# Another order of the same pieces: a layer norm, windowed attention and a GELU layer on one core

## The chip, the cores and the metric

The kernel runs on one core of a Trainium2 chip. The core has five engines with instruction streams of their own: TensorE (PE, matmuls), VectorE (DVE), ScalarE (ACT), GpSimd (POOL) and SyncE (SP), which here only issues DMA transfers. The metric is the device time of one execution in microseconds (us), smaller is better; the runs of the kernel before took 209.0 to 210.06 us, median 209.08.

## The reference

The input is x with 2048 rows of 640. It is normalised row by row, and the result goes two ways: through an attention with 32 heads of 20, in which each row looks at itself and seven earlier rows at a distance of two, and through a dense layer of 1536 with a tanh GELU. Both results and x are added.

```
xn = _layernorm(x)                                   # 2048 x 640
q, k, v = split(xn @ wqkv)                           # 32 heads of 20
logits[s, w] = q[s] . k[s - 2 w] * 20 ** -0.5        # w = 0..7, -1e9 where s - 2 w < 0
o[s] = sum over w of softmax(logits)[s, w] * v[s - 2 w]
A = o @ wo
B = gelu(xn @ w1 + b1) @ w2 + b2
return x + A + B
```

## The kernel before

The rows are cut into four chunks (n = 0 to 3) of 512 rows, each of four blocks (bl or j) of 128. Everything is held transposed, with features on the partitions and rows along the free dimension, so that a shift by a row is a shift of an address.

The work of a chunk is cut into pieces, each a small function under a short name. One string, ORDER, lists every piece once; the kernel runs through it and records each piece's instructions, and so each engine gets its instructions in the order of that string. No scheduler moves them later. An engine takes them strictly in that order, and waits at an instruction until its inputs are there and its target buffer is free. The names, with the digit of the chunk first:

- Loads on SP: `ldx` (the x rows of chunks 2 and 3, three transfers), `ld2` (w2, four), `ldo` (wo, three). The loads of chunks 0 and 1, of wqkv and of w1 are issued before the list begins.
- Layer norm: `st` (statistics on DVE, chunks 0 and 1), `su`, `sq` (row sums and squares on ACT, chunks 2 and 3), `rs`, `rc` (reciprocal of the deviation on ACT, mean times it on DVE), `xn` (the normalised rows; on ACT from chunk 1 on). Then `tc` turns a block: by PE and a copy in chunk 0, by a DMA transpose on SP from chunk 1 on (`do_td`).
- Projections: `hj`/`hc` (chunk 0, in pairs of blocks) and `pj`/`pc` (other chunks): `pj` is five matmuls of 512 columns on PE into an accumulator of the pool `psA`, `pc` the copy of it on ACT. The two digits behind the chunk are which of q, k, v (0, 1, 2) and which fifth of the features. `ga`, `gb`, `gd`, `ge` and `gc` are the first q columns, `pad` and `pk` carry 14 columns over from the chunk before.
- Attention on DVE: `qk` multiplies q of one block with the eight shifted k (one instruction of 5120 elements in each partition, 2.8 us), `pa`, `pb` add features up, `lg` sums over heads on PE into a PSUM tile L, `cp` copies it out (for chunk 0 half by ACT, `cp0a`, and half by DVE, `cp0b`), `m`, `mx`, `ex`, `ss`, `ri`, `at` are the softmax (largest value, subtraction, exponent, sum, reciprocal, product; `ex` and `ri` on ACT). `xe` spreads the weights of one block from 32 partitions to 128: a DMA on SP (`expand`), an expansion below. `av` multiplies them with the shifted v (again 2.8 us), `ac`, `ad`, `ot` add the eight positions up (of chunks 0 to 2, blocks 0 and 1 do `ac` by an accumulating DMA on POOL) and give oT.
- Dense layer: `f1` (five matmuls on PE into `psA`), `ge` (bias and GELU on ACT; it needs another table of functions than `ex`, `ri` and `rs`, so a table load of 1.28 us stands where the kind changes).
- Output of chunks 0 to 2: `t` (on PE into the pool `psO`; the last digit 0 to 3 are parts of gelu @ w2, three matmuls each, 4 is o @ wo, five matmuls, which needs oT), `u` (bias, ACT), `ut` (a DMA transpose back on SP, an output transpose below), `ud` (an accumulating DMA on POOL into the output, onto which `xp` has copied x). Chunk 3 is computed with rows on the partitions instead: `o3` (PE; last digit 4 needs oT), `dl`, `dh` (addition of x on DVE), `dd`, `dlo`, `dhi` (stores). `xb` adds b2 to the x rows of chunk 3. `ohi` is a last group of narrow matmuls.

The pool `psA` has four accumulators and serves `hj`, `pj`, `f1` and some of `o3`; `psO` has two and serves `t`. So a `pj` or `f1` on PE waits until ACT has emptied the accumulator that it gets, which is one used about four such pieces earlier.

The lines: 289 is the DMA transpose of `tc`, 125 the load of x rows, 153 of w2, 575 the expansion, 701 the output transpose, 612 `f1`, 331 `pj`, 694 `t`, 650 `o3`, 478 `lg`, 428 `qk`, 463 and 469 `pa` and `pb`, 582 `av`, 595 `ac`, 599 `ad`, 605 `ot`, 218 and 225 `su` and `sq`, 260 `xn`, 395 `pc`, 515 and 518 `cp`, 628 `ge`, 697 `u`, 706 `ud`, 593 `ac` by DMA, 170 the table load. The list is run here:

```
    with tc.manual_schedule(engines=engines):

        do_warm(WARM, CH)
        do_warm(3, P)
        assert sorted(ORDER) == sorted(pieces)
        for name in ORDER:
            pieces[name]()
```

Of the kernel before, what the change touches and what calls it, by code (L numbers as in the profile page):

```python
# [37 lines left out]
COLS = ((0, 2), (2, 4), (4, 5))  # L38

ORDER = """  # L40
sum1 st00a st00 wa rs00 xn00a wb tp00a neg1 xn00b tp00b tc00a tb sq1 ga tc00b rs01 gb2 mean1 xn01a tp01a gb3 xn01b
st03a tc01a st02a st02 tp01b gb4 gd st03 tc01b ge hj100 gc0 rs02 xn02 rs03 gc4 xn03 st11a gc1 hc100 st12a tp02 st13a
st10a tp03 st13 st10 hj102 st11 tc02 st12 tc03 hj101 pad01 hc101 hj111 hj112 hc102 hc111 rs1 rc1 xn13 hc112 pk b1
hj011 xn11 hj110 hj202 hj010 hc011 hc110 hj012 tc13 hc010 qk00 hc202 tc11 xn10 hj200 ldx f10_1 qk01 pa00 f10_2 hc012
qk03 ge0_1 f10_0 qk02 f10_3 ge0_2 xn12 ge0_0 f10_11 f10_5 hc200 ho pa01 ge0_3 ge0_11 tc10 tc12 su20 su22 pb01 f11_3
ge1_3 pj104 pj111 su21 pad11 pad02 pc104 su23 pj101 pc111 pj102 ng2 pc101 pj112 sq22 pj100 ge0_5 pb04 sq21 pj113 pc112
pj114 lg0 pc100 sq23 pc113 pc102 cp0a pj110 pc114 cp0b m0b pj103 xp2 hj210 ld2 hj201 xp0 mask mx0b m0a ex0b pc103 mx0a
pc110 ss0b pj121 sq20 qk10 rs2 hc210 pj122 f10_7 t000 ex0a hc201 ss0a rc2 xp1 f10_9 pc122 ri0b ri0a qk11 pc121 f10_4
ge0_4 su33 ge0_9 qk13 f10_6 t001 pj120 qk12 f11_5 xn23 ge0_7 pj124 ge0_6 su32 pc120 f11_10 xn20 f11_9 ldo t040 ge1_10
f10_8 pc124 su31 tc23 ge0_8 tc20 t041 xn21 hj211 pa10 at0a t002 su30 f11_0 tc21 hc211 xn22 ng3 pa11 at0b ge1_9 sq32  # L50
xe01 f11_1 pb11 t042 ge1_1 pb14 sq30 f10_10 hj212 ge0_10 lg1 t003 sq31 tc22 xe00 av01 cp1a pj202 hc212 pj214 xe02
ge1_0 pj204 ge1_5 sq33 pj210 av00 ac01 pc202 rs3 pc204 pj123 av02 t043 pc210 pj200 pj211 pc214 xe03 ac00 cp1b pc211
rc3 pc123 pj203 pj201 pc201 pj213 pj220 pc203 m1 pad12 mx1 pc200 av03 pad21 ac02 ex1 xn30 pc213 ss1 pj221 pj222 pc220
tc30 pc221 ac03 pj223 xn33 f12_10 ri1 at1 pc222 ad01 pj224 xe10 ad00 xn32 xe13 pc223 ot01 ot00 pj212 xe12 pc212 f11_4
av10 xe11 av12 f11_6 pc224 f11_8 av13 t004 ac10 ac13 tc32 t044 u00 t010 t011 t012 u04 t013 ut00 t014 ud00 av11 t020
xn31 t021 tc31 ac12 u01 t030 t022 ge1_8 t023 tc33 t024 f11_2 t031 ad11 ge1_4 ac11 t032 t033 ge2_10 pad22 ge1_6 t034
pj313 ot11 u03 qk22 pj312 pc313 qk23 pc312 pj324 ut01 ge1_2 ad10 u02 pj303 f11_7 pc324 pc303 ge1_7 t140 pj301 pj310
f12_1 ge2_1 ut02 t141 pc310 ot10 pa21 qk20 t130 f11_11 pj311 pc311 pc301 f12_2 pj304 pc304 qk21 pa20 t131 f13_2 ge1_11
pj300 pb21 pb24 pj302 ge2_2 pad31 pj314 pc302 t132 t142 pc314 t143 f13_8 pc300 f13_10 f12_0 lg2 pad32 t144 qk31 ut03
ut04 ud01 t133 cp2b t134 ud02 ge2_0 ud03 ge3_2 f13_1 cp2a u13 ge3_10 pj320 m2 qk30 t100 pc320 ge3_1 f13_5 qk32 pa30  # L60
t101 u14 ge3_5 xb mx2 f12_11 f12_8 qk33 t110 t111 t102 t112 f12_5 ge2_11 t113 t103 ex2 t104 ge2_5 u10 f12_4 ss2 ri2
ut10 t114 t120 t121 t122 pa31 at2 xe20 xe21 ge2_4 f13_7 pb31 u11 ge3_7 pj322 pc322 f12_3 pb34 f13_6 lg3 ge3_8 f13_4
xe22 ut11 cp3a ge2_3 ge3_6 t230 ge2_8 av21 av22 av20 f12_7 t123 f12_6 ge2_6 pj323 f13_0 ge3_4 xe23 t124 f12_9 pc323
ud10 f13_11 ge2_7 u12 ge3_0 ac21 t200 f13_3 ac20 av23 ge2_9 cp3b m3 mx3 ge3_11 o300 ge3_3 t201 ac22 ac23 ex3 ss3 o320
ri3 o301 ad21 ut12 t202 pj321 ud11 o321 t203 pc321 at3 xe30 ud04 xe31 ut13 o322 t231 t232 ot21 xe32 f13_9 ad20 ge3_9
ut14 ot20 t233 av30 o302 t204 xe33 u20 t234 t210 ut20 av31 t211 t212 o310 u23 t220 t213 t221 ud12 t222 t214 o323 u21
t223 t224 ac31 u22 av33 ac30 t240 o311 t241 av32 t242 ud13 ud20 o312 ad30 ut21 t243 t244 o313 ot30 o330 ud14 ac32 ac33
u24 ud21 ad31 ut22 o314 o331 ud22 o332 o303 o304 o333 ot31 o324 dh0 dl1 dh1 ut23 o334 ut24 ohi dl0 ud23 dh2 dd0 dl2
dl3 dd1 dd2 dh3 dlo ud24 dhi
""".split()  # L70


# [782 lines left out]
```

## Time and profile before

| | |
|---|---|
| median of 3 runs | 209.08 us (209.0 to 210.06) |
| the profiled execution | 209.62 us, its span 207.8 us |
| granted TensorE clock | 1.0 |
| ACT, 40 to 65 us | 23.34 us busy of 25 |
| PE, 40 to 65 us | 24.73 us busy of 25 |
| ACT, 152 to 205 us | 17.09 us busy of 53 |
| x rows, `ldx` (L125), issued | 19.39 us, three in 1.60 us |
| transposes of rows (L289), issue to landing | 2.4 / 4.0 / 6.4 us (least, median, most) |
| expansions (L575), issue to landing | 3.6 / 4.2 / 6.0 us |
| output transposes (L701), issue to landing | 2.3 / 3.3 / 6.2 us |
| loads of x (L125), issue to landing | 2.5 / 4.6 / 8.1 us |

The span runs from the first to the last instruction of the program; the rest of the execution's time lies around it. A row of the timeline gives the start and the duration in us, the engine, the line, what is written from what, a count, and in square brackets how long the engine sat idle before it and what ended that. A `q` behind an engine's name is its sequencer, which issues transfers. Idle time counts only where the engine is the one that the end waits for.

### The profile page before, as it was taken

To read this page: it belongs to the slowest core of one execution; us is meant where nothing else is said; L and a number is where in the kernel's file an instruction comes from. 1 tells how busy PE (TensorE), PEld (TensorE's weight loads), DVE (VectorE), ACT (ScalarE), POOL (GpSimd) and SP (SyncE) were. 2 spreads that over 40 slices of the span, in tenths; PEclk is the share of its full clock that TensorE was granted. 3 is DMA by queue.
4 is the path that set the end of the run, shared out by engine and by line. 5 is a ranking of instruction groups with operands and counts; after the bars stand their busy time and mean duration, and the time that the engine had idled before them with its cause. 6 is when DMAs were issued, how large, how long until landed. Compare 5 with 4: busy or idle time off the path is not lost.

```text
span 207.8 us, 2852 instructions
## 1 busy us (share of the span) xinstructions
PE 199.0 (96%) x1082; PEld 104.9 (50%) x1100; DVE 185.9 (89%) x161; ACT 126.6 (61%) x235; POOL 29.6 (14%) x40
## 2 busy tenths in 40 slices
PE   8999979999999999999999999999999998999793
PEld 3898435564454555444454454444444454444352
DVE  2989999499998998999999997999959999959993
ACT  5679969899989949547272532758964835211100
POOL 2000000000000400031407000000202630207420
PEclk9999999999999999999999999999999999999999
DMA  6996999800219691579597930000495994899963
GB/s 210 391 395 179 271 308 335 317 1 0 65 37 155 153 174 35 123 154 163 101 138 81 100 48 0 3 0 0 82 162 103 138 148 70 137 104 96 106 49 126
DMA packets 38430, 27.31 MB, mean 131 GB/s; under 512 B 25106, under 2 KB 34578, under 8 KB 38418
## 3 DMA queue, kind: packets, MB, share of 16 engines
q1 hardware_dynamic: 28016, 20.39, 39.2%
q0 software_dynamic: 10080, 6.56, 26.5%
q10 hardware_dynamic: 322, 0.20, 0.3%
q8 instruction: 8, 0.13, 0.3%
q14 instruction: 4, 0.03, 0.1%
HBM read 10.49 MB, written 4.59 MB: 73 GB/s over the span
## 4 chain that ended last, share of the span: by engine, by line
PE 50%; DVE 26%; DMA 8%; ACT 6%; SPq 5%; issue 3%; DVEq 0%
PE pps L331 19%; PE T L694 15%; PE hps L612 12%; DVE prod L582 7%; DVE prod L428 5%; DMA x_sb<-in_A_x_dram 4%; SPq L701 3%; DMA x_sb<-attn 3%; PE lo L650 3%; DVE prod L469 2%; DVE prod L463 2%; DVE prod L595 2%; DMA ax<-attn 2%; DVE stats L206 2%; ACT xn L260 1%
## 5 line engine op out<-in xcount | busy, mean ns | idle before, releaser
L612 PE MATMUL hps<-xnT,w_sb 128*128 128x512 bf16 x237 | 56.7, 379 | 1.7 <-ACT trash L218 1.5
L428 DVE TENSOR_TENSOR prod<-qT,kT 128x5120 bf16<-128x5120 bf16 x16 | 44.5, 2820 | 1.4 <-PE L L478 1.3
L694 PE MATMUL T<-hT,w_sb 128*128 128x512 bf16 x177 | 44.4, 379 | 0.2
L612 PEld LDWEIGHTS <-w_sb 128*128 128x128 bf16 x240 | 23.4, 98 | 29.8 <-issue 2.4
L628 ACT ACTIVATE hT<-hps,bT 128x512 bf16<-128x512 f32 x36 | 24.1, 689 | 11.2 <-PE hps L612 9.5
L706 POOL DMA_DIRECT2D out_dram<-x_sb x15 | 20.5, 1613 | 62.6 <-DMA x_sb<-x_sb 62.6
L694 PEld LDWEIGHTS <-w_sb 128*128 128x128 bf16 x180 | 17.2, 98 | 20.2 <-issue 0.4
L697 ACT ACTIVATE x_sb<-T,bT 128x512 bf16<-128x512 f32 x15 | 10.3, 687 | 24.4 <-PE T L694 22.5
L582 DVE TENSOR_TENSOR prod<-vT,x_sb 128x5120 bf16<-128x5120 bf16 x8 | 22.3, 2820 | 3.0 <-DMA x_sb<-attn 3.0
L582 DVE TENSOR_TENSOR prod<-vT,ax 128x5120 bf16<-128x5120 bf16 x8 | 22.1, 2820 | 3.1 <-DMA ax<-attn 2.4
L593 POOL DMA_DIRECT2D prod<-prod x6 | 7.3, 1220 | 106.2 <-DVE prod L582 106.2
L694 PE MATMUL T<-oT,wo 128*128 128x512 bf16 x73 | 17.9, 379 | 0.8 <-DVE oT L605 0.6
L469 DVE TENSOR_TENSOR prod<-prod 128x4096 bf16<-128x4096 bf16 x8 | 18.3, 2290 | 0.2
L463 DVE TENSOR_TENSOR prod<-prod 128x4096 bf16<-128x4096 bf16 x8 | 18.3, 2286 | 0.1
L331 PE MATMUL pps<-xnT,wk_sb 128*128 128x512 bf16 x73 | 18.2, 379 | 0.1
L331 PE MATMUL pps<-xnT,wq_sb 128*128 128x512 bf16 x72 | 18.0, 379 | 0.2
L331 PE MATMUL pps<-xnT,wv_sb 128*128 128x512 bf16 x72 | 17.7, 379 | 0.1
L170 ACT ACT_TABLE_LOAD x12 | 15.4, 1283 | 0.9 <-PEq L839 0.7
L595 DVE TENSOR_TENSOR prod<-prod 128x2560 bf16<-128x2560 bf16 x10 | 14.7, 1485 | 0.1
L331 PEld LDWEIGHTS <-wk_sb 128*128 128x128 bf16 x75 | 8.7, 118 | 7.6 <-issue 0.4
L331 PEld LDWEIGHTS <-wq_sb 128*128 128x128 bf16 x75 | 8.8, 117 | 7.5
L331 PEld LDWEIGHTS <-wv_sb 128*128 128x128 bf16 x75 | 8.8, 117 | 7.3
(96 smaller groups left out, 241.7 us busy)
## 6 DMA issues: line engine op xcount, KB each, us to landing
prod<-prod POOLq DMA_DIRECT2D x6, 640.0 KB, 6.6
ax<-attn SPq DMA_DIRECT2D x8, 256.0 KB, 4.1
x_sb<-attn SPq DMA_DIRECT2D x8, 256.0 KB, 4.6
w_sb<-in_B_w_dram SPq DMA_DIRECT2D x2, 960.0 KB, 11.0
out_dram<-x_sb SPq DMA_DIRECT2D x3, 640.0 KB, 9.3
w_sb<-in_B_w_dram SPq DMA_DIRECT2D x4, 480.0 KB, 7.7
out_dram<-x_sb POOLq DMA_DIRECT2D x15, 128.0 KB, 5.4
x_sb<-in_A_x_dram SPq DMA_DIRECT2D x2, 640.0 KB, 7.2
```

The source lines that it names most:

```text
L170: nc.scalar.preload_act_table_set(name)
L331: nc.tensor.matmul(ps[:], lhsT=wqkv_p[which][:, ti, to, :], rhs=xnT[:, ti, :], start=(ti == 0), stop=(ti == KT - 1),)
L428: nc.vector.tensor_tensor(out=prod[:, j], in0=q[:, :, at].unsqueeze(1).to_broadcast([P, W, KT, P]), in1=window(k, at), op=ALU.mult,)
L463: nc.vector.tensor_tensor(out=low, in0=low, in1=high, op=ALU.add)
L469: nc.vector.tensor_tensor(out=first, in0=first, in1=rows[:, :, t * P : (t + 1) * P], op=ALU.add)
L582: nc.vector.tensor_tensor(out=prod[:, j], in0=window(qkv_tile(n, 2), slice(j * P, (j + 1) * P)), in1=ax_view(n)[:, j, :, :].unsqueeze(2).t ...
L595: nc.vector.tensor_tensor(out=low, in0=low, in1=high, op=ALU.add)
L612: nc.tensor.matmul(ps[:], lhsT=w1_sb[:, ti, ft * P : (ft + 1) * P], rhs=tiles["xnT", n][:, ti, :], start=(ti == 0), stop=(ti == KT - 1),)
L628: nc.scalar.activation(hT, tiles["hps", n, ft][:], ACT.Gelu_apprx_tanh, bias=bT[:, ft : ft + 1], scale=1.0)
L694: nc.tensor.matmul(ps[:], lhsT=lhs, rhs=rhs, start=pc == 0 and k == 0, stop=pc == 4 and k == len(srcs) - 1)
L697: nc.scalar.activation(take("straight", n, s), tiles["T", n, s][:], ACT.Identity, bias=bT[:, FT + s : FT + s + 1])
L706: nc.gpsimd.dma_start(dst, src, accum_op=ALU.add)
```

## The change

ORDER is replaced by another order of the same names. No function, tile, size or buffer is changed, and each engine executes the same instructions but one: the functions' table is loaded once more on ACT (13 times instead of 12). The diff replaces the whole string; what stands in it on the engines that the prediction speaks of is this, each engine's own pieces in their order, old (-) and new (+):

```diff
 SP, first part
-tc13 tc11 ldx tc10 tc12 xp2 ld2 xp0 xp1 ldo tc23 tc20 tc21 xe01 tc22 xe00 xe02 xe03
+tc11 tc13 tc12 tc10 ldx ld2 tc20 xp1 tc23 xe00 xe01 tc21 tc22 xe02 xe03 xp2 xp0 ldo
 SP, second part
-tc30 xe10 xe13 xe12 xe11 tc32 ut00 tc31 tc33 ut01 ut02 ut03 ut04 ut10 xe20 xe21 xe22 ut11 xe23 ut12
+xe10 xe11 xe13 xe12 tc32 tc30 ut00 ut01 tc31 tc33 ut02 ut03 ut04 ut10 xe22 xe20 xe21 ut11 xe23 ut12
-xe30 xe31 ut13 xe32 ut14 xe33 ut20 ut21 ut22 ut23 ut24 dd0 dd1 dd2 dlo
+xe30 xe31 ut13 xe33 ut14 ut20 xe32 ut21 ut22 ut23 ut24 dd1 dd2 dd0 dlo
 ACT, chunk 1's rows
-rs1 xn13 hc112 pk xn11 hc011 hc110 hc010 hc202 xn10 hc012 (table) ge0_1 ge0_2 xn12 ge0_0 hc200 ge0_3 ge0_11 su20 su22
+rs1 hc110 pk xn11 hc111 xn13 hc010 hc011 xn12 hc200 xn10 (table) ge0_11 ge0_2 pad11 ge0_1 hc201 ge0_5 su20 ge0_3 pc110 pc111 su22
 ACT, 39 to 52 us
-cp0a pc114 (table) ex0b pc103 pc110 sq20 rs2 hc210 ex0a hc201 pc122 ri0b ri0a pc121 (table) ge0_4
+cp0a (table) ex0b pc100 pc114 pc101 sq21 ex0a ri0b pc121 pc124 sq23 pc123 ri0a sq20 hc202 rs2 hc210 pc120 (table) ge0_4
 ACT, chunk 3's rows
-xn30 pc213 pc220 pc221 xn33 ri1 pc222 xn32 ... u04 xn31 u01 (table) ge1_8 ge1_4 ge2_10 pad22 ge1_6 u03
+xn32 pc220 pc211 u00 xn30 u04 pad22 xn31 u01 pad31 (table) ge1_2 u03 ge1_7 ge2_1 pad32 xn33 ge1_4
 ACT, last softmax
-(table) ex3 ri3 pc321 (table) ge3_9
+(table) ex3 (table) ge2_9 ge3_3 ge2_11 pc321 pc322 (table) ri3 pc323
 PE, from f10_1 to lg0
-f10_1 f10_2 f10_0 f10_3 f10_11 f10_5 f11_3 pj104 pj111 pj101 pj102 pj112 pj100 pj113 pj114 lg0
+f10_1 f10_11 hj201 f10_2 f10_5 pj110 f10_3 pj102 pj111 pj112 pj103 pj104 f10_0 pj114 pj113 lg0
 PE, the end
-t204 t234 t210 t211 t212 o310 t220 ... t244 o313 o330 o314 o331 o332 o303 o304 o333 o324 o334 ohi
+t204 t234 t210 t211 t212 t220 ... t244 o311 o312 o313 o304 o330 o331 o314 o324 o332 o333 o334 ohi
 DVE, first logits
-pb04 cp0b m0b mask mx0b m0a mx0a ss0b qk10 ss0a rc2 qk11 qk13 qk12 pa10 at0a pa11 at0b pb11 pb14
+pb04 cp0b m0b mx0b mask m0a ss0b mx0a qk13 ss0a qk10 at0b qk11 rc2 qk12 at0a pa11 pa10 pb11 pb14
 DVE, last two chunks
-av21 av22 av20 av23 m3 mx3 ac22 ac23 ss3 ad21 at3 ot21 ad20 ot20 av30 av31 ac31 av33 ac30 av32 ad30 ot30 ac32 ac33 ad31 ot31
+av22 av21 m3 mx3 av20 ss3 ac22 av23 at3 ac23 ad21 ad20 ot21 ot20 av30 av31 ac31 av33 ac30 ad30 av32 ot30 ac33 ac32 ad31 ot31
```

In the list itself `cp0a` stands ahead of `cp0b` before and behind it after. The order on POOL changes in one place: `ud00` is issued ahead of `ac10` instead of behind it.

## The prediction

> **What bounds the kernel now.** I read the page's busy shares first, then the chain of waits, then the timeline around each place where TensorE (PE) stands still, and last the same places on VectorE (DVE), ScalarE (ACT) and the SP queue. From the page:
>
> ```profile
> PE 199.0 (96%) x1082; PEld 104.9 (50%) x1100; DVE 185.9 (89%) x161; ACT 126.6 (61%) x235; POOL 29.6 (14%) x40
> ...
> PE 50%; DVE 26%; DMA 8%; ACT 6%; SPq 5%; issue 3%; DVEq 0%
> ...
> L612 PE MATMUL hps<-xnT,w_sb 128*128 128x512 bf16 x237 | 56.7, 379 | 1.7 <-ACT trash L218 1.5
> ```
>
> A 512-column matmul is shown as 379 ns, but consecutive ones begin closer together, as the chain of waits shows:
>
> ```profile
> 85.35 3.24 PE hps L612 x15
> 88.59 6.69 PE T L694 x31
> ```
>
> 3.24/15 and 6.69/31 are 216 ns each. The same reading of consecutive starts gives 109 ns for 256 columns, 56 ns for 128, and 69 ns per logit matmul. The program issues 788, 125, 118 and 32 of these, beside 24 transposes, bias and late warm-up matmuls: 170.1 + 13.6 + 6.6 + 2.2 + 1.6 = 194.0 us. This total is the same in both kernels, and PE takes it in the written order. So I lay the work ahead of a piece against the moment at which it starts; the difference is the time PE has lost so far. In the trace of before it is 5.5 us at the first transpose, 5.8 at f10_1 (19.96), 7.7 at lg0 (38.04), 7.9 at t004 (88.2), 8.2 at lg2, 8.2 at t204, 8.8 at t244, 10.5 at o314 (195.65) and 10.6 at the end. From t004 to lg3 PE loses 0.4 us in 64. Outside the start, then, it stands still in three places.
>
> PE in the timeline, around 28, 176 and 196:
>
> ```profile
> 28.24 1.02 PE L612 MATMUL hps<-xnT,w_sb 128*128 128x512 bf16 x4 [1.53 <-ACT trash L218]
> ...
> 176.28 1.89 PE L694 MATMUL T<-oT,wo 128*128 128x512 bf16 x8 [0.56 <-DVE oT L605]
> ...
> 195.65 0.39 PE L650 MATMUL lo<-wo,oT 128*128 128x512 bf16 x1 [1.33 <-DVE oT L605]
> ```
>
> The first is f11_3, the first piece that reads all of chunk 1's transposed rows. ACT is named, but its buffer was free at 24.7. What ended last was the fourth transpose. SP and ACT:
>
> ```profile
> 21.10 4.23 SPq L289 DMA_TRANSPOSE xnT<-xn  x2
> ...
> 23.18 0.92 ACT L260 ACTIVATE xn<-x_sb,nmr,rstd 128x640 bf16<-128x640 bf16 x1
> ```
>
> xn12 stands behind a table load and two gelus on ACT, ends at 24.1, and tc12 is issued up to 25.3. The other two places wait for oT from DVE, and DVE itself waits there for expansions stuck behind output transposes on SP:
>
> ```profile
> 177.40 0.60 SPq L575 DMA_DIRECT2D x_sb<-attn  x1
> 178.11 2.16 SPq L701 DMA_TRANSPOSE x_sb<-x_sb  x1
> 180.31 0.59 SPq L575 DMA_DIRECT2D x_sb<-attn  x1
> ...
> 186.30 2.83 DVE L582 TENSOR_TENSOR prod<-vT,x_sb 128x5120 bf16<-128x5120 bf16 x1 [2.19 <-DMA x_sb<-attn]
> ```
>
> **The change, part by part.** Nothing is added but one table load on ACT (1.28 us, the L170 row). The rest is a permutation, so I walk the new order with the durations of the old trace (ACT from start to start: copy 0.47, xn 0.81, gelu 0.57, row sum 0.84, square 0.9; DVE: 2.73 a 5120 product, 2.2 to 2.3 a 4096 one, 1.4 a 2560 one). Where two engines meet I take the later.
>
> *Head, 15 to 36 us.* ACT now runs xn11, xn13, xn12, xn10 ahead of the table load: they end at about 17.1, 18.4, 20.3 and 21.6 with the projection copies between. SP issues tc11, tc13, tc12, tc10 directly behind them (1.2 each), the last up to 22.8. The shortest landing of these transposes is 2.4 us from issue, the longest 6.4. Nothing else loads then, since the x rows wait behind and the w1 halves land before 19; I take 24.0 (by the longest, 28.0). PE reaches pj110, the new first user, at 24.8: the 1.7 us stall goes. By the longest landing 3.2 us come instead. The moved loads (three issues, 1.6 us) go out at 22.8 to 24.4 instead of 19.4 to 21.0, and behind them ld2, tc20 and everything later on SP. Their first reader is su20 on ACT at 26.4; queued behind su20 are ge0_3 and pc110, which free the buffers of pj112 (29.1) and pj103, so rows landing by 27.7 cost nothing. Their landings lie between 2.5 and 8.1 us from issue, that is 25.3 to 30.9; I take the lower part, 27, because these rows now leave right behind the transposes with nothing loading before them.
>
> lg0 thus stands at 29.8 us of work + 5.8 + 0.25 = 35.85, against 38.04. DVE has its input (pb04) at 15.75 + 4x2.73 + 2x2.2 + 2x2.3 = 35.7, so it doesn't hold it. Behind lg0, DVE copies its half before ACT does; before, it came second:
>
> ```profile
> 39.33 0.69 DVE L518 CAST e<-L 128x512 bf16<-128x512 f32 x1 [3.21 <-ACT e L518]
> ```
>
> That is 0.6 us less between logits and softmax.
>
> *Middle, 36 to 152 us.* ACT is the tight one up to 52 (23.34 us busy of 25 in the window 40 to 65). Walking both, f10_4 waits 0.45 us for hc202, f11_10 0.25 us for ge0_4 behind a table load; lg1 stands at 63.5 (before 64.8), pb14 being ready at 63.0. ot00 is ready at 86.4 and t004 wants it at 87.2. Chunk 3's xn33 now waits behind pad32, hence for av11 (98.8): its transpose is issued at 100.9 to 102.1 and lands by 104, or 107.3 by the longest row; pj310 wants it at 105.7, so 0 to 1.6. At lg2 (126.5) DVE is early (pb24 124.7) and idles some 2.5 us: this gives back DVE's lead but costs PE nothing, as PE has other work. lg3 follows at 152.0.
>
> *Tail.* DVE starts on chunk 2's values at 152.6 (before 154.4). m3, mx3 now come between av21 and av20 and at3 ahead of ac23, ad21: at3 ends at 169.0 instead of 173.2. The added table load stands ahead of ri3, behind pc322: pj322 ends at 165.5, copy, load and the two small exponents at 168.0. DVE's av23, up to 168.3, hides it; without that cover at3 would be up to 1.3 us later. xe30, xe31 leave at once, ut13 takes 1.2, xe33 leaves at 171.6 instead of 180.3. DVE wants it at 182.1, and the longest landing of an expansion is 6.0. Only xe32 stays behind ut20, whose source needs t204 and u20: issued by 179.1, landed by 185.1 even at 6.0, wanted at 187.7. Both waits of DVE for expansions go; ot20 ends at 175.0 (t204 wants it at 175.2), ot30 at 191.3 (o304: 192.5), ot31 at 196.5 (o324: 196.5).
>
> **The sum.** PE's loss at the end falls from 10.6 to 5.8 + 0.25 + 0.7 + about 0.5 around the logits and oT = 7.3 us: 3.3 less. Several handovers have under half a microsecond of slack (f10_5, hj202, pj221, ot20, ot31), so I give back 0.7: 2.6 us. If all keep their slack and the 0.5 vanishes too, it is 3.8, hence 205.3; if tc33 and the transposes of chunk 1 take their longest landings, 1.6 + 3.2 eat the gain. The profiled execution took 209.62, span 207.8: it would be 207.0, span 205.2. It stands 0.54 above the median of the runs, 209.08, so the median becomes **206.5**. The tail behind the last matmul (3.1 us) stays.
>
> One rule speaks for another limit: the Trainium skill, "Perfetto Trace Analysis", section "Identifying the Most-Contended Engine", says that busy matmul time tells little and that the share of weight loads should be read. Here that is 50%, so by it PE has room and DVE (89%) is the limit. The 216 ns from start to start, kept for 60 us on end, disagrees.
>
> **Rivals.**
> - *DVE alone is the limit.* Then the end moves as DVE's last oT does: 200.8 to 196.5, so 204.8. For it: DVE's 89%. Against it: PE's work behind that oT grows by o332 and o333 (2x0.65), and PE loses 0.4 us in the middle. 0.06.
> - *The tail's waits return.* xe32 late by over 2.6 us, or t204 and o304 arriving on oT as before, brings back the 0.56 + 1.5: 208.6. For it: ot20 and ot31 have no slack. 0.14.
> - *ACT is overfull between 24 and 52 us.* Each of its delays passes to PE through four accumulator buffers; another 1.5 us there: 208.0. For it: 93% busy. Against it: the walk leaves most copies 0.3 to 1 us early. 0.12.
> - *The later x rows stop ACT: slower.* If the first rows land as the big loads at 29 to 34 us do (9.4 us from issue at most: xp1), su20 waits until 32.8, ge0_3 ends at 34.3, and pj112, due at 29.1, loses 5.2 us, with DVE behind it through lg0: 211.7. It decides from a landing at 30.3 on, where it has eaten the 2.6. Against it: the weight loads are issued behind these rows. 0.11. On this the Trainium skill, "DMA: Bandwidth & Descriptors", section "Queues, rings and completion order", says that each DMA engine takes one queue's descriptors in ring order; by that the weights couldn't overtake. The old order, rows ahead of ld2, shows no wait of su20.
>
> **Chances.** The forecast has 0.57, with 204.8 to 208.0 as its own range. About 0.5% (1.05 us) is what can be told from no change. Faster (under 208.0): 0.55 of the forecast, 0.06, half of ACT's 0.12 and 0.02 of the tail's = 0.69. Slower (over 210.1): 0.11 and 0.01 = 0.12. The same: 0.19. The range 204.8 to 209.4 leaves out the slow rival and a little at the lower end.
>
> **What would show it.** Right: no PE gap over 0.5 us between 24 and 30; lg0 before 36.5; the first copy of L by DVE, without a 3 us wait; an idle DVE of 2 to 3 us before the first product behind lg2; no wait of L582 for x_sb<-attn over 1 us; the last oT before 197.5; SP's expansions of x_sb at 169 to 172. Wrong: su20 (L218 after 26) waiting for x_sb<-in_A_x_dram; a PE gap at the first L331 near 25 or near 105; a wait for oT over 1 us in the last 15 us.

## The result, and the profile after

The changed kernel takes 212.34 us (median of 6 runs, 211.8 to 216.35), the kernel before 209.29 in the runs beside it (208.27 to 210.85). The ratio is 1.0137, 95% interval 1.0092 to 1.0182: slower by 1.4%, where 1.2% faster was forecast.

The first profiled execution of the changed kernel, 216.35 us, was disturbed from its start on, so I read a second one of the same kernel (a0_same, 212.83 us, span 211.1, granted clock 0.983), against the 209.62 us and span 207.8 of before.

> The changed kernel itself, once more. In its trace PE has lost 9.1 us of time by hj101 (5.8 before), stands 4.6 us ahead of pj310 for the transpose tc33, and then runs some 5 us at half the clock. Theory (one late transpose): the head's 3 us belong to that execution alone, so here PE has lost about 6 us at lg0, and 13 to 14 at the end; wait ahead of pj310 4 to 5 us, then starts 432 ns apart; 212.3 us. Rival (the later x loads and the new head cost it): 9 us lost by lg0 again, and most of the difference to before stands ahead of lg0.

Its four executions had a median of 212.41, ratio 1.0157 [1.0103, 1.0210]. From its page: the busy row, the granted clock in 40 slices of 5.3 us, the chain of waits by engine, and two groups of instructions (behind the bar: busy us, mean ns, idle us before them).

```profile
PE 201.9 (96%) x1081; PEld 105.8 (50%) x1100; DVE 186.6 (88%) x161; ACT 128.6 (61%) x236; POOL 29.7 (14%) x40
...
PEclk9999999999999999999975999999999999999999
...
PE 83%; DMA 9%; ACT 3%; DVE 2%; SPq 1%; issue 1%; ACTq 0%
...
L428 DVE TENSOR_TENSOR prod<-qT,kT 128x5120 bf16<-128x5120 bf16 x16 | 44.7, 2820 | 9.1 <-PE L L478 8.9
...
L331 PE MATMUL pps<-xnT,wk_sb 128*128 128x512 bf16 x74 | 19.9, 413 | 4.2 <-DMA xnT<-xn 4.1
```

PE is still 96% busy, and DVE and ACT as before. Three things are new: one idle time of 4.1 us on PE, which a row transpose ended; a clock of 0.7 and 0.5 in the slices 21 and 22 (from 106 us on), where it was 0.9 or more throughout; and 8.9 us in which DVE waited for logits. DVE's part of the chain fell from 26% to 2%: PE alone sets the end now. The place is the first piece that reads chunk 3's transposed rows, pj310. The timeline of PE (start, duration, in brackets the idle time before):

```profile
99.84 5.56 PE L612 MATMUL hps<-xnT,w_sb 128*128 128x512 bf16 x24
109.50 4.43 PE L331 MATMUL pps<-xnT,wk_sb 128*128 128x512 bf16 x10 [4.11 <-DMA xnT<-xn]
...
117.06 1.24 PE L331 MATMUL pps<-xnT,wk_sb 128*128 128x512 bf16 x5
```

Ten matmuls that begin 216 ns apart elsewhere take 4.43 us here. By their records they start 427 ns apart and last 634 ns each. The table by stretches (length; busy us and count of PE, PEld, DVE, ACT, POOL; granted clock; the load on the DMA engines; GB/s) shows how long that lasts:

```profile
106.00:110.00 4.00, 0.50 (x2) 0.27 (x3) 4.00 (x3) 0.78 (x2) 0.13 (x1) 0.80 1.61 147
110.00:116.00 6.00, 6.00 (x18) 2.19 (x17) 5.96 (x4) 1.76 (x3) 3.78 (x3) 0.57 0.83 74
116.00:120.00 4.00, 3.95 (x19) 2.13 (x19) 3.97 (x2) 0.00 (x0) 0.00 (x0) 1.00 1.02 100
```

18 matmuls in 6 us at a clock of 0.57, then 19 in 4 us at 1.00. The 0.57 is the mean of the stretch: the granted clock is 0.50 from 108.38 to 115.21 us, 6.83 us long, and 1.00 on both sides. In the ledger of the prediction (start of a piece less the work ahead of it) the loss is 5.7 at pj110, 6.0 at lg0, 6.3 at lg1, 10.6 at pj310, 12.2 at t140, 13.2 at t131, 13.5 at lg2, 13.6 at lg3 and 13.5 at the end. So 4.1 us go in the wait. What the low clock costs can be read from the timeline: 22 matmuls start from 109.50 to 117.06, which is 7.56 us where 216 ns each make 4.75, so 2.8 us (13.2 - 10.6 in the ledger gives 2.6). Outside this place PE loses less than in the kernel before: 1.7 less at lg0, and nothing from lg3 to the end, where it lost 2.4 from lg2 on. The whole loss rises from 10.6 to 13.5, by 2.9. PE's last matmul ends at 207.91 instead of 204.69, 3.2 later, and the span rose by 3.3, so the ledger is good to about 0.3 us.

The SP queue shows the head, the transposes of chunk 3 and the tail:

```profile
16.95 6.07 SPq L289 DMA_TRANSPOSE xnT<-xn  x4
23.07 1.60 SPq L125 DMA_DIRECT2D x_sb<-in_A_x_dram  x3
...
95.97 6.52 SPq L289 DMA_TRANSPOSE xnT<-xn  x2
...
175.50 1.20 SPq L575 DMA_DIRECT2D x_sb<-attn  x2
177.21 2.23 SPq L701 DMA_TRANSPOSE x_sb<-x_sb  x1
179.50 0.59 SPq L575 DMA_DIRECT2D x_sb<-attn  x1
```

Chunk 1's four transposes leave in one go and the x rows behind them, as written. The last one, tc33, begins to be issued at 100.54 and ends at 102.49 (95.97 + 6.52). Which transfers ran beside it: rows of the transfers issued from 95 to 104 us (KB each, median us from the start of the issue to landing; of the two transposes only tc33's landing is recorded):

```profile
prod<-prod POOLq DMA_DIRECT2D x2, 640.0 KB, 7.9
out_dram<-x_sb POOLq DMA_DIRECT2D x2, 128.0 KB, 6.8
xnT<-xn SPq DMA_TRANSPOSE x2, 8.8
```

The two `prod` transfers are ac10 and ac11, the accumulating additions on POOL; the other two are the stores ud00 and ud01. POOL issued them in this order:

```profile
93.77 1.30 POOL L706 DMA_DIRECT2D out_dram<-x_sb  x1 [21.51 <-issue]
94.54 1.74 POOL L593 DMA_DIRECT2D prod<-prod  x1
98.82 1.20 POOL L593 DMA_DIRECT2D prod<-prod  x1 [2.54 <-DVE prod L582]
99.54 1.81 POOL L706 DMA_DIRECT2D out_dram<-x_sb  x1
```

ud00 landed at 97.92, before tc33 was issued. ac10 landed at 101.93, ac11 at 107.13, ud01 at 109.00, and tc33 at 109.37, 8.8 us from the start of its issue. So ac11 and ud01 ran beside tc33 for most of that time, and ac10 for its first 1.4 us. DVE, last:

```profile
133.82 2.83 DVE L428 TENSOR_TENSOR prod<-qT,kT 128x5120 bf16<-128x5120 bf16 x1 [8.86 <-PE L L478]
...
188.37 2.82 DVE L582 TENSOR_TENSOR prod<-vT,x_sb 128x5120 bf16<-128x5120 bf16 x1
```

The wait of 8.86 us is the mark of lg2 coming 6.6 us later (133.1 against the forecast 126.5). The second line is av33: the 2.2 us wait for an expansion that stood there is gone.

### The profile page after: what moved, and what is told of

Same layout as the page of the kernel before. It is cut to its first block, busy times and chain, and to the rows that moved or that the text cites. A ratio compares the mean times of both kernels' runs of the same rounds, so it can differ in the third digit from the quotient of the medians.

```text
span 214.6 us, 2853 instructions
## 1 busy us (share of the span) xinstructions
PE 203.2 (95%) x1081; PEld 107.2 (50%) x1100; DVE 186.8 (87%) x161; ACT 129.0 (60%) x236; POOL 29.7 (14%) x40
## 4 chain that ended last, share of the span: by engine, by line
PE 88%; DMA 8%; ACT 1%; issue 1%; SPq 0%; DVE 0%
PE T L694 24%; PE pps L331 24%; PE hps L612 22%; PE gps L375 6%; PE lo L650 5%; DMA xnT<-xn 4%; DMA wq_sb<-in_A_wqkv_dram 3%; PE both L650 2%; PE gps L344 2%; PE hi L650 1%; PE L L478 1%; PE tp L277 1%; ACT hT L628 0%; ACT xn L260 0%; ACT x_sb L697 0%
## 5 line engine op out<-in xcount | busy, mean ns | idle before, releaser
L612 PE MATMUL hps<-xnT,w_sb 128*128 128x512 bf16 x235 | 55.7, 379 | 0.3
L331 PE MATMUL pps<-xnT,wk_sb 128*128 128x512 bf16 x74 | 19.9, 413 | 4.6 <-DMA xnT<-xn 4.6
L593 POOL DMA_DIRECT2D prod<-prod x6 | 7.9, 1400 | 91.2 <-DVE prod L582 76.4
L395 ACT CAST kT<-pps 128x512 bf16<-128x512 f32 x15 | 8.8, 587 | 10.9 <-PE pps L331 10.9
L395 ACT CAST qT<-pps 128x512 bf16<-128x512 f32 x15 | 8.7, 584 | 7.8 <-PE pps L331 7.8
```

The source lines that it names most:

```text
L331: nc.tensor.matmul(ps[:], lhsT=wqkv_p[which][:, ti, to, :], rhs=xnT[:, ti, :], start=(ti == 0), stop=(ti == KT - 1),)
L395: nc.scalar.copy(dest[:, to, off : off + CH], tiles["pps", n, which, to][:])
L612: nc.tensor.matmul(ps[:], lhsT=w1_sb[:, ti, ft * P : (ft + 1) * P], rhs=tiles["xnT", n][:, ti, :], start=(ti == 0), stop=(ti == KT - 1),)
```

## The experiments

My theory after the result: the head and the tail gained what was forecast, and the whole loss comes from tc33, first by its wait and then by the clock that falls during it. Rivals: that the low clock is a disturbance of its own; that the wait costs little because DVE's lead takes it; that the new order as a whole, with ACT or DVE overfull, is what is slower. The runs of before beside the next ones have medians of 208.90 to 209.05.

**Chunk 3's rows late in the old order** (b1_xn33_late). If tc33 alone makes the loss, the old order should lose the same when its xn33 and tc33 are moved to where the new order has them.

```diff
-tc30 pc221 ac03 pj223 xn33 f12_10 ri1 at1
+tc30 pc221 ac03 pj223 f12_10 ri1 at1
...
-xn31 t021 tc31 ac12 u01 t030 t022 ge1_8 t023 tc33 t024
+xn31 t021 tc31 ac12 u01 t030 t022 ge1_8 t023 t024
...
-ge2_10 pad22 ge1_6 t034
+ge2_10 pad22 ge1_6 xn33 tc33 t034
```

> The kernel before with xn33 moved on ACT from 82 us to behind ge1_6 (101), and tc33 with it; the same order on PE, DVE and POOL. Theory: tc33 is issued at 102 to 103, beside ac11 and ud01, lands at 108 to 110, pj313 (102.45) waits 5 to 8 us and the clock halves for some 5 us: 7 to 10 us slower than before, 216 to 219. Rival (tc33 lands 2.4 to 4 us from its issue, as the median of these transposes does): it waits 2 to 3 us, no fall of the clock, 211 to 212.

216.15 us, ratio 1.0349 [1.0303, 1.0396]. PE's timeline and a stretch behind the wait:

```profile
107.42 4.43 PE L331 MATMUL pps<-xnT,wk_sb 128*128 128x512 bf16 x10 [4.69 <-DMA xnT<-xn]
```

```profile
107.00:113.00 6.00, 5.58 (x15) 2.06 (x16) 5.96 (x4) 1.69 (x4) 1.30 (x1) 0.54 0.32 26
```

The wait is here too, and the clock falls (0.50 from 105.70 to 112.53): the loss goes from 7.9 to 12.8 and on to 15.4 at lg2. A disturbance that comes by itself would not follow the edit into another order.

**xn33 early in the new order** (a1_xn33_early, and once more beside later runs, a1_again). On ACT xn33 goes directly behind xn31; SP's order stays.

```diff
-av12 xn31 tc30 ut00 ud00 ac10 u01
+av12 xn31 xn33 tc30 ut00 ud00 ac10 u01
...
-f12_2 f12_3 pad32 xn33 ge1_4 ge2_2
+f12_2 f12_3 pad32 ge1_4 ge2_2
```

> The changed kernel with one instruction moved: xn33 on ACT directly behind xn31, so that tc33 follows tc31 on SP at about 101 instead of 104 to 106. Theory (tc33 issued late costs its wait and the clock behind it, 7.2 us together): the wait ahead of pj310 goes or shrinks below 1 us, the clock stays at 1.0, lg2 comes 6 to 7 us earlier: 205.2 us, at most 207. Rival (the landing is slow because of POOL's accumulating transfers whenever it is issued): tc33 lands 8 us behind its issue, at 109 to 110, 1 to 2 us of waiting stay: 207 to 209. Rival (loss elsewhere): 212.

> The changed kernel with xn33 early once more, beside the other three on one chip: 206.0, 1.2 to 1.5% faster than before; PE's lost time 6.1 to 6.5 us from pj310 to the end, no wait over 0.5 us.

205.98 us, ratio 0.9892 [0.9832, 0.9952], and 206.79, 0.9893 [0.9855, 0.9931]. From the first one, PE and the transfers issued from 95 to 104 us:

```profile
99.66 5.56 PE L612 MATMUL hps<-xnT,w_sb 128*128 128x512 bf16 x24
105.06 2.33 PE L331 MATMUL pps<-xnT,wk_sb 128*128 128x512 bf16 x10
```

```profile
prod<-prod POOLq DMA_DIRECT2D x2, 640.0 KB, 7.8
out_dram<-x_sb POOLq DMA_DIRECT2D x1, 128.0 KB, 9.5
xnT<-xn SPq DMA_TRANSPOSE x2, 7.8
```

tc33 is issued 3.4 us earlier, still needs 7.8 us, and lands at 104.93, just in time for a start at 105.06; the ten matmuls take 2.33 us. PE's loss is 6.3 at the end (8.1 in a1_again, whose first weights came 1.0 us late and whose tc33 made PE wait 0.7). One piece of 0.9 us on ACT, moved, turns the change from 1.4% slower to 1.1% faster: nothing else of the new order has to be slow.

**The wait filled with matmuls** (a2_fill). 20 matmuls of ones into a PSUM tile nobody reads stand ahead of pj310, so that PE waits for the rows without being idle. They are work added to the kernel.

```diff
-ge1_6 tc33 pj310 u02
+ge1_6 tc33 wc pj310 u02
...
+    def do_fill(n):
+        spare = psL.tile([P, W, P], F32, tag="L", name="spare")
+        for _ in range(n):
+            nc.tensor.matmul(
+                spare[:].rearrange("p w c -> p (w c)")[:, 0:CH],
+                lhsT=ones[:, 0:P],
+                rhs=ones[:, 0:CH],
+                start=True,
+                stop=True,
+            )
...
+    piece("wc", do_fill, 20)
```

> The changed kernel with 20 matmuls of 512 columns of ones ahead of pj310 (4.3 us at 216 ns), into a logit tile that nobody reads: extra work, nothing left out. If the fall of the clock behind the idle stretch is a cost of its own: starts of pj310 216 ns apart, 2.0 to 2.7 us less than the changed kernel, 209.8. If only the wait for tc33 costs time, or the clock falls for another reason: 212.3, within 0.4.

211.63 us, ratio 1.0140 [1.0103, 1.0177]. PE, and the stretch that ran at 0.57 without the filling:

```profile
105.56 4.54 PE L716 MATMUL spare<-const-bfloat16-1.0 128*128 128x512 bf16 x20
110.56 2.33 PE L331 MATMUL pps<-xnT,wk_sb 128*128 128x512 bf16 x10 [0.47 <-DMA xnT<-xn]
```

```profile
110.00:116.00 6.00, 5.48 (x26) 2.78 (x27) 5.97 (x4) 1.65 (x3) 3.92 (x3) 1.00 0.86 89
```

The clock stays at 1.00 and the ten matmuls take 2.33 us, with the rows as late as before. So the low clock is a consequence of idle PE. But only 0.8 us of the expected 2.0 to 2.7 show in the median (1.8 in the span): tc33 landed about 1 us later still, at 110.43, and the repair gives part of it away. There was also less to win than the trace suggests. The other three executions of a0_same had mean clocks of 0.991 or 0.992, the traced one 0.983. By estimate, (1 - 0.992) x 2 x 210.5, the clock was at half for about 3.4 us in them, not 6.8; they have no trace. Filling treats the smaller part of the loss.

**Why tc33 is slow.** Two runs of the changed kernel take the POOL transfers from beside it. In c2_ac_dve the additions of chunk 1 are DVE instructions, as in chunk 3:

```diff
-BY_DMA = ((0, 1), (0, 1), (0, 1), ())
+BY_DMA = ((0, 1), (), (0, 1), ())
```

> The changed kernel with chunk 1's two additions ac10 and ac11 done by VectorE instead of POOL's transfers (two instructions of 1.4 us more on DVE, which idles some 9 us at lg2). If these two transfers stretch tc33's landing: it lands 1.2 to 3 us from its issue, at 104 to 105.5, PE waits under 1 us, no fall of the clock: 206 to 207.5. If ud00 and ud01 do: 211 to 213. Rival: DVE's 2.8 us are not free and lg2 comes later: 208 to 209 though the wait is gone.

In c1_ud_late the two stores ud00 and ud01 move behind ud02 on POOL. This does more than it was meant to: ac10 no longer stands behind ud00 and leaves earlier.

```diff
-tc30 ut00 ud00 ac10 u01
+tc30 ut00 ac10 u01
...
-ut02 ut03 ut04 pj303 pc303 pc313 ud01 ud02 pj320
+ut02 ut03 ud02 ud00 ut04 pj303 pc303 pc313 ud01 pj320
```

> The changed kernel with two accumulating output transfers on POOL, ud00 and ud01, moved behind ud02, so that neither runs beside tc33; ac10 and ac11 stay where they are. tc33 lands 6.9 us from the end of its issue in the changed kernel, 1.2 where nothing else moves. If POOL's small output packets stretch it: it lands at 104 to 106, 3 to 5 us less with the clock: 208 to 209. If ac10 and ac11 (640 KB each) do: it lands within 1 us of where it did, 109, and the time is 212, within 0.5.

c2: 208.14 us, ratio 0.9969 [0.9946, 0.9991]. c1: 206.98 us, 0.9911 [0.9884, 0.9938]. The transfers issued from 95 to 104 us, of c2 and then of c1:

```profile
out_dram<-x_sb POOLq DMA_DIRECT2D x2, 128.0 KB, 3.9
xnT<-xn SPq DMA_TRANSPOSE x2, 2.4
```

```profile
prod<-prod POOLq DMA_DIRECT2D x1, 640.0 KB, 6.3
xnT<-xn SPq DMA_TRANSPOSE x2, 5.2
```

POOL's issues in c1:

```profile
89.30 1.20 POOL L593 DMA_DIRECT2D prod<-prod  x1 [16.96 <-DVE prod L582]
98.91 1.20 POOL L593 DMA_DIRECT2D prod<-prod  x1 [8.41 <-DVE prod L582]
```

There ac10 had landed at 95.75, so ac11 alone (landed at 105.18) ran beside tc33. The same transpose, issued at about the same moment (101.6 in c2, 100.6 in c1), needs 8.8 us beside ac10, ac11 and ud01, 5.2 beside ac11 alone, and 2.4 in c2 without additions, where ud01 landed at 102.81. So the transfers of POOL make it late. How much of the 3.6 us between 8.8 and 5.2 is ud01's and how much ac10's, these runs do not separate. Neither kernel lets the clock fall; pj310 waits 0.5 in c1 and not at all in c2. c2 does not gain the rest, as PE shows (the rival of its expectation came out):

```profile
105.73 2.32 PE L331 MATMUL pps<-xnT,wk_sb 128*128 128x512 bf16 x10
...
128.42 0.61 PE L478 MATMUL L<-prod,head_of 128*32 128x512 bf16 x8 [1.81 <-DVE prod L469]
```

The additions on DVE push its products back, and lg2 waits 1.8 us for them. c1 came out better than I expected.

**tc33 ahead of the output transpose on SP** (c6_tc33_first): a1 with tc31 and tc33 moved ahead of tc30, ut00 and ut01. A miss.

```diff
-av12 xn31 tc30 ut00 ud00 ac10 u01
+av12 xn31 xn33 tc31 tc33 tc30 ut00 ud00 ac10 u01
...
-ut01 tc31 f12_2 f12_3 pad32 xn33 ge1_4
+ut01 f12_2 f12_3 pad32 ge1_4
...
-ge1_6 tc33 pj310
+ge1_6 pj310
```

> The changed kernel with xn33 early and tc31, tc33 ahead of the first two output transposes on SP. In a1_xn33_early tc33 landed at 104.9, just when PE wanted it. Here it is issued at 95 to 98 and lands by 102 even with 5 us: the same time as a1_xn33_early within 0.5 in the median, 206, with less spread. If the output transposes behind it are late for ut04 or u03: up to 1 us slower.

210.28 us, ratio 1.0052 [1.0014, 1.0089]. tc33 landed at 98.23, long ahead of need. POOL and DVE show what it cost:

```profile
101.34 1.30 POOL L706 DMA_DIRECT2D out_dram<-x_sb  x1 [28.06 <-issue]
102.11 2.97 POOL L593 DMA_DIRECT2D prod<-prod  x2
```

```profile
113.22 1.49 DVE L599 TENSOR_TENSOR prod<-prod 128x2560 bf16<-128x2560 bf16 x1 [3.81 <-DMA prod<-prod]
```

ut00 now leaves at 98.35, so ud00 goes out at 101.34 where it was 93.56 in a1. Both additions stand behind ud00 in POOL's order, though they do not need it: ac10, which left at 89.30 in c1, leaves at 102.11. ac11 lands at 113.1, DVE waits 3.8 us for it, and PE 2.8 at lg2.

**The x rows back ahead of chunk 1's last transposes** (c3_ldx_back): a1 with `ldx` at its old place.

```diff
-tc13 qk00 xn10 ge0_11
+tc13 ldx qk00 xn10 ge0_11
...
-ge0_5 ldx qk02 pj110
+ge0_5 qk02 pj110
```

> The changed kernel with xn33 early (206.0), and the x loads put back ahead of chunk 1's last two transposes tc12 and tc10. If moving the loads is what frees pj110 of its wait: tc10 lands 2.7 to 5 us from the end of its issue instead of 1.2, at 26 to 28 instead of 24.0, PE waits 1.5 to 3 us ahead of pj110, later than 206.0 by 1 to 3 us: 207 to 209. If only the order on ACT (xn12 ahead of the table load) did it: 206.0, within 0.5.

212.38 us, ratio 1.0126 [1.0048, 1.0203]; a1 takes 206 to 207. PE and SP of its profiled execution, which was the shortest of its four (209.58 us):

```profile
28.50 1.25 PE L331 MATMUL pps<-xnT,wk_sb 128*128 128x512 bf16 x5 [3.53 <-DMA xnT<-xn]
```

```profile
19.31 1.60 SPq L125 DMA_DIRECT2D x_sb<-in_A_x_dram  x3
21.01 2.74 SPq L289 DMA_TRANSPOSE xnT<-xn  x2
```

Behind the x rows, tc12 and tc10 land at 27.84 and 28.41, 5.5 and 4.7 us after the end of their issue, against 1.17 each in front of them. PE waits 3.5 us. The clock did not fall in this execution (0.999). The three others, at mean clocks of 0.992, 0.991 and 0.984, took 212.07, 212.68 and 215.32; these have no trace, so that the clock fell in them, at this wait, is likely and not shown. More came than I expected: the wait alone is 3.5 us where I had 1.5 to 3, and for the clock I had nothing.

**The two gains by themselves, in the old order.** The head (d1_head): xn12 directly behind xn10 on ACT, and tc10, tc12 ahead of the x rows on SP.

```diff
-tc11 xn10 hj200 ldx f10_1
+tc11 xn10 xn12 tc10 tc12 hj200 ldx f10_1
...
-ge0_2 xn12 ge0_0
+ge0_2 ge0_0
...
-ge0_11 tc10 tc12 su20
+ge0_11 su20
```

> The kernel before with the head's part of the change alone: xn12 on ACT directly behind xn10, tc10 and tc12 ahead of the x loads on SP. Theory: the 1.7 us wait ahead of f11_3 goes, lg0 at 36.4 instead of 38.0, and PE keeps that to the end: 1.3 to 1.7 us faster than before, 207.3. Rival (lost again, since DVE or oT sets the last 60 us): the same as before within 0.5, 208.9.

207.64 us, ratio 0.9948 [0.9927, 0.9969]. PE's timeline around 28 and at the end:

```profile
23.73 4.26 PE L612 MATMUL hps<-xnT,w_sb 128*128 128x512 bf16 x19
27.83 1.24 PE L331 MATMUL pps<-xnT,wq_sb 128*128 128x512 bf16 x5
...
192.97 0.39 PE L650 MATMUL lo<-wo,oT 128*128 128x512 bf16 x1 [0.74 <-DVE oT L605]
```

The wait at f11_3 is gone, and lg0 stands at 36.55 instead of 38.04. The tail (d2_tail) is the exchange of two expansions on SP:

```diff
-ot21 xe32 f13_9
+ot21 xe33 f13_9
...
-t204 xe33 u20
+t204 xe32 u20
```

> The kernel before with one exchange from the tail's part of the change alone: xe33 and xe32 swap places on SP, so that the expansion that DVE wants first is not behind ut14. Theory: DVE's 2.2 us wait ahead of av33 goes, ot30 comes 1.5 to 2.2 us earlier, the wait ahead of o314 (1.3 to 1.7) goes: 207.4. Rival (PE's work or ot31 sets the end anyway): within 0.5 of before, 208.9.

207.91 us, ratio 0.9947 [0.9923, 0.9970]. SP's wait moves to the expansion that is needed later; DVE begins av33 at 184.25 instead of 186.30 and without waiting, and o314 finds its oT:

```profile
184.25 2.82 DVE L582 TENSOR_TENSOR prod<-vT,x_sb 128x5120 bf16<-128x5120 bf16 x1
```

Both edits together (d3_both, the two diffs above):

> The kernel before with both parts, head (as d1_head) and tail (as d2_tail). If PE's lost time adds up over the two waits: 208.9 - 1.3 - 1.4 = 206.2. If DVE, earlier after the head, no longer waits at the tail, or meets another wait: as d1_head, 207.6.

207.02 us, ratio 0.9908 [0.9876, 0.9940], and PE's loss at the end is 6.8 instead of 10.6. Within the intervals the gains add up: 0.52% and 0.53% by themselves, 0.92% together. Two small edits in the old order are worth almost what the whole new order with a1's repair is worth.

## Why the prediction was wrong

- **What bounds the kernel** was right. Loss by loss on PE moved the end: the head's wait, the tail's, and the new one in the middle each showed up in the time in d1, d2, d3 and a1. DVE alone as the limit (one rival) fell: from lg2 on PE waited for nothing of DVE's (loss 13.5 there and 13.5 at the end), while DVE stood 8.9 us for PE's logits, 6.4 more than forecast. DVE still has little to spare: 2.8 us more work on it in c2, and a late addition in c6, came back to PE at lg2. For that rival the prediction cited the Trainium skill, "Perfetto Trace Analysis", section "Identifying the Most-Contended Engine", which names MFU (the work done as a share of the peak) beside the share of weight loads; the prediction read the second alone. Its own 194 us of matmul starts in a span of 207.8 spoke for PE.
- **The head** was right to 0.2 us up to lg0, and to 0.5 at lg1: tc10 landed at 24.18 (24.0), lg0 stood at 35.79 (35.85), lg1 at 63.0 (63.5). The x rows landed at 26.35, 27.18 and 30.82; su20 waited 0.15 us for the first, and PE for none. So the slower rival that I priced, x rows that stop ACT, did not come. The section of the Trainium skill cited there ("DMA: Bandwidth & Descriptors", "Queues, rings and completion order") lets a later transfer finish its write before an earlier one, so "couldn't overtake" says more than it does; here the first part of w2 landed at 32.04, after the last x rows. c3 shows the old place in this order costs more than I had given it: PE's stall there was 3.5 us, not the 1.7 of before.
- **The tail** was right: no wait of av33 or av32 for an expansion, no wait of PE for oT, and no loss from lg3 to the end. The rivals "the tail's waits return" and "ACT is overfull" did not come. All of it lay later by the middle's loss: ot31 ended at 202.8, 6.3 behind the forecast.
- **The step that failed** is this one: "Chunk 3's xn33 now waits behind pad32, hence for av11 (98.8): its transpose is issued at 100.9 to 102.1 and lands by 104, or 107.3 by the longest row; pj310 wants it at 105.7, so 0 to 1.6". The issue was right to 0.4 us (100.5 to 102.5). The landing was 109.4: 8.8 us from the issue, beyond the longest of before (6.4), which I had taken for a bound. Only six of the twelve transposes of before have a recorded landing, and tc33 is not among them. In the old order tc33 was issued up to 97.4, ahead of ac11 and ud01 (101.0 and 101.7), for a reader at 102.67 that never waited; the new order issues it behind ac11 and ud01, with ac10 still under way, and c1 and c2 show that such neighbours make it slow. The exchange of ud00 and ac10 on POOL, which the prediction does not price, is why ac10 was still there: it left at 94.54, and at 89.30 in c1. A range of a transfer's times holds for the neighbours it had. The price is 4.1 us, where the sum took 0.
- **A term was missing**: the clock. The wait of 4.1 us cost another 2.8 behind it in the traced execution; a2 and b1 show that the low clock follows from the wait. 4.1 + 2.8, less the gains of 1.7 and 2.4 in head and tail, makes 2.8 of the 2.9 us by which PE's loss rose.
- **The size of the gain** was right where the failed step is taken out. a1, the new order with xn33 early, takes 205.98 and 206.79; the forecast was 206.5. That it is so close is in part luck: the sum held 0.7 us that was a guess, and the start of the kernel alone differs by 0.8 us between the two traces of a1.

## What to carry to other kernels

When an order of work moves a transfer, look up which other transfers are under way at its new time: its duration in the old trace belongs to its old neighbours. A transfer that TensorE waits for needs slack for them, here 7.8 to 8.8 us from its issue instead of 2.4, and the cheap place to find it was upstream, in the small instruction that makes its source. Price a stall of TensorE of about 4 us with the slow matmuls behind it, here at 2.8 us on top of 4.1.

## What the runs showed of the hardware

- A transpose of 128x640 through DMA landed 1.2 us after the end of its issue with no addition beside it (tc10, tc12, and tc33 in c2), 3.2 us after beside one accumulating addition of 640 KB (c1), and 4.9 to 7.6 beside two of these in turn and an accumulating store (a1, a1_again, a0_same, a2_fill). The longest recorded total in the kernel before was 6.4 from the start of the issue.
- During idle times of PE of 4.1, 4.7 and 4.6 us (a0_same, b1, and the first execution of the changed kernel) the granted clock fell to 0.50, each time 3.0 us after PE stopped, and stayed there for 6.83 us; matmuls of 512 columns began 427 ns apart instead of 216. After 3.5 us (c3's profiled execution), 2.8 (c6) and 1.5 (before) it did not fall. In the three traces with a fall, every change of the clock up to the last matmul lies a whole multiple of 3.413 us behind the first record of the full clock. The three idle times that let it fall began 0.35 to 0.45 us behind such a point and so filled 3.0 us of one step; c3's is cut into 1.5 and 2.0 us by it. So the place of a wait may matter as well as its length; no run here moves a wait of one length to show it. The Trainium skill, "TensorE: Matmul & The Clock Gate", section "HAM oscillation — how this bites in real kernels", says that an idle time of over some 3.4 us sends the clock to half and that the next matmuls run slow. The traces agree: 4.1 us fell; that 3.5 us once did not lies within what the page's section "What's actually happening" says of a window of 3413 ns that runs freely.
- POOL issues its transfers in order, and one that waits for its source holds those behind it that do not: ac10 left at 102.11 in c6 and at 89.30 in c1, and c6 lost 3.8 us of DVE's time.
